# A gated block in three blocks of 1024 columns in place of four batches of 768

## The chip, the cores and the metric

One NeuronCore of a Trainium2 chip runs the whole kernel; the other cores are idle. The metric is the device time of one execution in microseconds. Engines are named as in the profile: PE (TensorE, matmuls), PEld (its weight loads), DVE (VectorE), ACT (ScalarE), POOL (GpSimd), SP (SyncE). POOL and SP only issue DMAs here, apart from some filling at the start.

## The reference

```
B, H, S, D = 4, 8, 768, 64                       # batches, heads, sequence, head size
q_bucket, k_bucket = hash bits of q @ proj, k @ proj          # 6 bits each
scores = where(q_bucket == k_bucket, q @ k^T / sqrt(D), -1e9)
attn   = softmax(scores) @ v                                  # (B, H, S, D)
x      = attn.transpose(0, 2, 1, 3).reshape(B * S, H * D)     # (3072, 512)
g      = x @ w_gate                                           # (3072, 1536)
out    = (g * sigmoid(g)) * (x @ w_val) @ w_out               # (3072, 512)
```

The inputs of attention are float32, the three weight matrices are float64 and are read as pairs of 32-bit words. Output: float32, 3072 x 512.

## The kernel before

**Attention** goes over 16 pairs of heads, numbered from 0: four pairs to a batch (`NP = 4`), since two heads of 64 rows fill the 128 partitions. For a pair n it issues the 24 score products (`score`, line 473), whose exponentials ACT writes to the ring of tiles `A` (476); DVE adds them up (`add`, 509 to 516); then come the products with v (`attend`, 487), which leave the pair's x, transposed, in a tile `xT` of 128 rows by 768 columns. The sums are taken a pair later, inverted, and spread over the partitions by two DMAs (`invert`, `r<-sums`); `norm` (551) then scales `xT`. For batches 1 to 3 the scaled x is stored to DRAM (`kept_x`, profile name `xram`, 556); for batch 0 it is split on the spot. The last pair's x is normed only in the next stage. From pair 4 on, q and k are transposed by DVE (440) and reloaded by four DMAs each (297), and the hash bits of q are copied to a second set of rows by a DMA (`qb<-qb`, 416). SP carries these DMAs in order.

In between, **pieces of the weights** are made: 36 pieces of 128 x 512, each from float64 words (`words`) by two ACT and three DVE operations (130 to 149) in a tile `stage`, then one ACT and two DVE operations (137 to 159), and stored to DRAM (`ram`, 161). 23 pieces are made during attention, the other 13 during the first batch of the next stage, by `turn`, whose steps are spread over the atoms of that stage.

**Three parts.** [...] Each operand is split into a high part h, a low part l, and a difference d. The sum of hh' and ll' goes to one PSUM tile (`a`, or the first bank of `o`), dd' to another (`n`, or the second bank), and the result is 4097 a - n. For x, `split` makes the parts: h by ACT (244), l and d by DVE (247, 251), each over 768 columns.

**The gated block** follows, with all x transposed: the token columns stream through PE and the weights are the stationary operand in the up products. For each batch b and each group f of 128 hidden columns (12 groups), `U` makes gate and value: `up` issues for both 2 x 4 x 2 matmuls into `a` and 2 x 4 into `n`, each over half a batch, 384 columns (`first`, `second`; every matmul of the stage is recorded at line 643). ACT evicts `a` (685), DVE subtracts `n` (691), ACT applies Silu (693), DVE multiplies (695), ACT rounds the product to h (696); l and d of the hidden tile `hid` follow on DVE (`tail`, 699, 701), issued after the next atom's matmuls. `D` takes three groups of `hid` at a time as stationary operands and streams three tiles of `w_out`, 512 columns wide: nine matmuls for each of six chunks of 128 tokens, into the two banks of one `o` tile. The first of the four `D` of a batch is evicted by ACT (738) and DVE (744), the others by DVE alone (740, 744); the last one's results go out by SP (746).

All PSUM is four tiles of two banks (`pp`), used in turn. Weight tiles come back from `ram` into two rings of four and three slots (`bring`, 233, POOL's queue), one load when an up product is done with its slot and three after a `D`.

The order of work is written out in the list `order`: `U` for all groups of all batches, each `D` placed after the `U` that follows the third of its groups. So the last `D` of a batch stands behind the first `U` of the next. Each `U` yields four atoms and each `D` six. The x of the next batch is loaded on SP (`load_x`, 769), two pairs before the batch's third `D` and two before its last two `U`, and split one step at a time in its last two groups. Only the very last `D` starts four of its chunks with the two older groups (`ahead`).

[...]

## Time and profile before

| | |
|---|---|
| runs | 946.80, 946.83, 948.48 us, median 946.83 |
| profiled execution | 948.66 us, span of its instructions 946.80 |
| PE, PEld, DVE, ACT, POOL busy | 927.0, 720.1, 665.1, 474.1, 112.4 us |
| first up matmul of the gated block | at 331.94 us |
| last down product | 929.35 to 941.79 us |
| mean granted clock of PE | 0.996 |
| DMA moved | 203.2 MB |

A row of operations has the line, engine and operation, output and inputs by the program's names, and sizes. A piece of the chain has its start, its length and what it was; a row of the timeline has the same and, in brackets, how long the engine had been idle and what ended that. A row by stretch has the stretch, its length, the busy time of PE, PEld, DVE, ACT and POOL with their instructions in brackets, the granted clock as a share of full speed, the mean share of the DMA engines, and GB/s.

### The profile page before, as it was taken

The numbers are of one execution on the slowest core, as the hardware profiler recorded it, in microseconds if no ns is written. First come the engines' busy times: TensorE is split into PE (matmuls) and PEld (weight loads), VectorE is DVE, ScalarE is ACT, GpSimd is POOL, SyncE is SP. The second block draws the span as 40 slices with busy tenths as digits, with TensorE's granted clock in tenths as the row PEclk, the third lists the DMA queues.
The fourth block names the chain that finished last, engine by engine and source line by source line (L and its number), as shares of the span: only waits on it lengthen the run. The fifth ranks groups of instructions, "written<-read, shape, count | busy, mean of one in ns | idle before, by whom it ended". The sixth has DMA issues, their size and how long they took to land.

```text
span 946.8 us, 14452 instructions
## 1 busy us (share of the span) xinstructions
PE 927.0 (98%) x5413; PEld 720.1 (76%) x5413; DVE 665.1 (70%) x804; ACT 474.1 (50%) x882; POOL 112.4 (12%) x223
## 2 busy tenths in 40 slices
PE   8999999999999989999999999999999999999997
PEld 4444445444444489999979999989999988999996
DVE  5566999989888738898975365676545667546466
ACT  6899878887888535535323332242331331332311
POOL 3011010001101110111011101111011011110100
PEclk9999999999999999999999999999999999999999
DMA  6466677887896598889758555467465465753741
GB/s 168 120 194 181 182 176 202 192 195 211 220 222 190 199 363 308 324 305 380 283 211 308 194 170 209 164 215 279 167 241 191 169 225 174 260 192 134 249 152 67
DMA packets 135797, 203.21 MB, mean 215 GB/s; under 512 B 92912, under 2 KB 100560, under 8 KB 135728
## 3 DMA queue, kind: packets, MB, share of 16 engines
q0 software_dynamic: 27696, 144.33, 42.8%
q1 hardware_dynamic: 107232, 57.77, 22.2%
q8 instruction: 43, 0.70, 0.3%
q10 hardware_dynamic: 800, 0.20, 0.1%
q14 instruction: 26, 0.21, 0.1%
HBM read 162.01 MB, written 39.42 MB: 213 GB/s over the span
## 4 chain that ended last, share of the span: by engine, by line
PE 84%; DVE 7%; ACT 4%; DMA 3%; issue 1%; SPq 0%; ACTq 0%; DVEq 0%; POOLq 0%
PE a L643 23%; PE o L643 19%; PE sc L473 15%; PE av L487 12%; PE n L643 12%; ACT A L476 1%; PE hps L399 1%; DVE xparts L247 1%; PE sum L527 1%; DMA r<-sums 1%; DMA xram<-xT 1%; DVE o L740 1%; DVE v L695 1%; DVE v L691 1%; ACT xparts L244 1%
## 5 line engine op out<-in xcount | busy, mean ns | idle before, releaser
L643 PE MATMUL a<-xparts,ring 128*128 128x384 f32 x1536 | 285.5, 336 | 7.9 <-ACT g L685 2.9
L643 PEld LDWEIGHTS a<-xparts,ring 128*128 128x128 f32 x1536 | 269.2, 188 | 12.0 <-ACT xparts L244 3.7
L643 PE MATMUL o<-ring,hid 128*128 128x512 f32 x864 | 199.5, 390 | 0.0
L643 PEld LDWEIGHTS o<-ring,hid 128*128 128x128 f32 x864 | 161.8, 188 | 33.6 <-DVE o L744 0.5
L476 ACT ACTIVATE A<-sc 128x384 f32<-128x384 f32 x384 | 157.4, 492 | 12.0 <-PE sc L473 12.0
L473 PE MATMUL sc<-qT,kT 64*128 64x384 f32 x768 | 158.7, 491 | 0.0
L643 PE MATMUL n<-xparts,ring 128*128 128x384 f32 x768 | 149.7, 335 | 1.1 <-DVE xparts L251 1.1
L233 POOL DMA_DIRECT2D ring<-ram x144 | 76.3, 532 | 509.8 <-PE n L643 317.9
L643 PEld LDWEIGHTS n<-xparts,ring 128*128 128x128 f32 x768 | 134.8, 188 | 2.0 <-DVE xparts L251 2.0
L487 PE MATMUL av<-A,vraw 128*64 128x386 f32 (+1 forms) x768 | 127.7, 488 | 0.0
L691 DVE TENSOR_TENSOR v<-v,n 128x768 f32<-128x768 f32 x48 | 45.7, 953 | 97.8 <-PE n L643 92.6
L685 ACT ACTIVATE g<-a 128x768 f32<-128x768 f32 x48 | 38.8, 809 | 141.3 <-PE a L643 141.3
L487 PEld LDWEIGHTS av<-A,vraw 128*64 128x64 f32 x768 | 53.7, 136 | 73.3 <-issue 64.0
L473 PEld LDWEIGHTS sc<-qT,kT 64*128 64x128 f32 x768 | 68.7, 188 | 50.2 <-issue 49.0
L696 ACT ACTIVATE hid<-v 128x768 fp32r<-128x768 f32 x48 | 40.7, 847 | 124.7 <-DVE v L695 118.9
L693 ACT ACTIVATE g<-g 128x768 f32<-128x768 f32 x48 | 40.7, 847 | 93.6 <-DVE g L691 93.6
L744 DVE TENSOR_TENSOR o<-o 128x512 f32<-128x512 f32 x90 | 61.8, 687 | 19.4 <-ACT o L738 17.1
L509 DVE SCALAR_TENSOR_TENSOR both<-A 128x1536 f32<-128x1536 f32 x32 | 56.1, 1754 | 18.3 <-ACT A L476 17.9
L473 PE MATMUL sc<-qb,kb 64*128 64x384 bf16 x384 | 64.7, 325 | 3.2 <-DMA qb<-qb 2.2
L691 DVE TENSOR_TENSOR g<-g,n 128x768 f32<-128x768 f32 x48 | 45.5, 948 | 30.2 <-PE n L643 28.7
L699 DVE SCALAR_TENSOR_TENSOR hid<-hid,v 128x768 fp32r<-128x768 f32 x48 | 45.9, 955 | 22.6 <-ACT hid L696 22.3
L740 DVE SCALAR_TENSOR_TENSOR o<-o 128x512 f32<-128x512 f32 x72 | 49.5, 688 | 13.9 <-PE o L643 13.1
(79 smaller groups left out, 727.9 us busy)
## 6 DMA issues: line engine op xcount, KB each, us to landing
ring<-ram POOLq DMA_DIRECT2D x144, 768.0 KB, 5.9
ram<-stage POOLq DMA_DIRECT2D x23, 768.0 KB, 4.9
ram<-stage SPq DMA_DIRECT2D x13, 768.0 KB
vraw<-in_v_dram SPq DMA_DIRECT2D x16, 384.0 KB
out_dram<-o SPq DMA_DIRECT2D x24, 256.0 KB
r<-sums SPq DMA_DIRECT2D x30, 192.0 KB
qraw<-in_q_dram SPq DMA_DIRECT2D x48, 96.0 KB
words<-in_moe_w_gate_dram POOLq DMA_DIRECT2D x9, 512.0 KB, 8.2
```

Source lines behind the costliest of these rows:

```text
L233: nc.gpsimd.dma_start(t.bitcast(FP32), ram[at].bitcast(FP32))
L473: nc.tensor.matmul(sc[h], x["k", n][rows, ks], x["q", n][rows, qs], start=start, stop=not start)
L476: nc.scalar.activation(weights(u)[:, h, 0:HQ], sc[h], AF.Exp, scale=SCALE * (OFF / 2 if n <= NP else 1.0))
L487: nc.tensor.matmul(ps[h * D : (h + 1) * D, 0:width], raws["v", n][:, h, c, :], a[:, h, 0:width], start=c == 0, stop=c == NCH - 1)
L509: nc.vector.scalar_tensor_tensor(out=t, in0=first, scalar=S * EPS / P / 2, in1=now, op0=ALU.add, op1=ALU.add)
L643: nc.tensor.matmul(ps, w, x, start=start, stop=stop)
L691: nc.vector.tensor_tensor(two(z), two(z), n_, op=ALU.subtract)
L693: nc.scalar.activation(z, z, AF.Silu)
L696: nc.scalar.activation(h, val, AF.Copy, scale=TOWARD / STEP)
L699: nc.vector.scalar_tensor_tensor(out=l, in0=h.bitcast(FP32), scalar=-STEP, in1=val, op0=ALU.mult, op1=ALU.add)
L740: nc.vector.scalar_tensor_tensor(out=accs[c], in0=t[:, 0], scalar=STEP + 1, in1=accs[c], op0=ALU.mult, op1=ALU.add)
L744: nc.vector.tensor_tensor(accs[c], accs[c], t[:, 1], op=ALU.subtract)
```

## The change

The columns of all batches (3072) are cut into three blocks of 1024 that run over the ends of batches; a block stands where a batch stood in the gated block. All up matmuls become 512 columns wide, and all elementwise work of an up group 1024. A `D` has eight chunks. A block's last `D` follows its last `U` directly, and every such `D` starts four chunks ahead with the two older groups; of the last block alone the other four chunks do their second product first, as before.

The parts of x now lie as two halves of 512 columns with the three parts inside. Block 0 holds batch 0 and the first 256 columns of batch 1, split during attention. For later blocks, `load_x` gathers 1024 columns from the two batches; pairs 0 and 1 are split in the last two `U` of a block, pairs 2 and 3 inside its last `D`. Their tiles take the place of block 0's parts or of the two weight stages, which now hold two pieces each.

The rings have three and three slots. The last pair's x has a tile of its own, and the spread sums for it go into an output tile. The steps of `turn` are drawn from one stream (`turns`). Pools are opened in another order, so buffers of the gated block lie elsewhere. What is scored, hashed and attended is unchanged.

```diff
+    WB = 2 * PIECE
+    NB = B * S // WB
...
-    stagep = [ctx.enter_context(tc.tile_pool(name="stagep", bufs=3))]
+    stagep = ctx.enter_context(tc.tile_pool(name="stagep", bufs=2))
...
-    even_x = ctx.enter_context(tc.tile_pool(name="even_x", bufs=1))
-    odd_x = {NP - 1: ctx.enter_context(tc.tile_pool(name="odd_x", bufs=1))}
-    RINGS = (4, 3)
+    xparts_p = ctx.enter_context(tc.tile_pool(name="xparts", bufs=1))
+    lastp = ctx.enter_context(tc.tile_pool(name="lastp", bufs=1))
+    RINGS = (3, 3)
...
+    def turns():
+        while progress["kept"] < NPIECE:
+            yield from turn()
...
-    for f in range(B * NF):
-        order.append(("U", f))
-        if f % NQ == 0 and f:
-            order.append(("D", f // NQ - 1))
-    order.append(("D", B * NF // NQ - 1))
+    for block in range(NB):
+        for f in range(NF):
+            order.append(("U", block * NF + f))
+            if f % NQ == 0 and f:
+                order.append(("D", (block * NF + f) // NQ - 1))
+        order.append(("D", (block + 1) * NF // NQ - 1))
...
+    def split(x, block, pr, first, count):
+        if (block, pr) not in xparts:
+            x_home(block, pr)
+        t = xparts[block, pr]
+        spans = []
+        at = 0
+        while at < count:
+            half, to = divmod(first + at, PIECE)
+            if to == 0 and (count - at) % PIECE == 0:
+                n = count - at
+                spans.append((x[:, at : at + n].rearrange("p (x t) -> p x t", t=PIECE),
+                              [t[:, half : half + n // PIECE, i] for i in range(3)]))
+            else:
+                n = min(PIECE - to, count - at)
+                spans.append((x[:, at : at + n], [t[:, half, i, to : to + n] for i in range(3)]))
+            at += n
...
         def low():
+            for x_, (h, l, d) in spans:
+                nc.vector.scalar_tensor_tensor(out=r32(l), in0=h, scalar=-STEP, in1=x_, op0=ALU.mult, op1=ALU.add)
...
-            else:
-                later.extend(split(x, b, pr, even_x))
+            if b * S < WB:
+                later.extend(split(x, 0, pr, b * S, min(S, WB - b * S)))
...
     def gated_block(scope):
         ringp.append(scope.enter_context(tc.tile_pool(name="late_ring", bufs=RINGS[1])))
-        rest = scope.enter_context(tc.tile_pool(name="odd_x_rest", bufs=1))
+        gatep = scope.enter_context(tc.tile_pool(name="gatep", bufs=2))
         hidp = scope.enter_context(tc.tile_pool(name="hidp", bufs=4))
-        gatep = scope.enter_context(tc.tile_pool(name="gatep", bufs=2))
         outp = scope.enter_context(tc.tile_pool(name="outp", bufs=1))
...
-                for half in halves_():
+                for half in range(WB // PIECE):
                     for j in range(NJ):
                         for v in range(2):
-                            mm(a[:, half, 0:HQ], block(v, j), xparts[b, j][:, v, halves[half]],
+                            mm(a[:, half], block(v, j), r32(xparts[b, j][:, half, v]),
...
-                    for go in (second, first) if final else (first, second):
+                    for go in (second, first) if final and c >= ahead else (first, second):
...
-                ahead = 4 if final else 0
+                ahead = 4 if part == NF // NQ - 1 else 0
...
+        def load_x(block, prs):
+            ...
+                while at < (block + 1) * WB:
+                    b, col = divmod(at, S)
+                    n = min(S - col, (block + 1) * WB - at)
+                    nc.sync.dma_start(x[:, to : to + n], kept_x[b, pr][:, col : col + n])
+        def split_x(block, pr):
+            return split(raw_x.pop((block, pr)), block, pr, 0, WB)
...
+                elif kind == "U" and f >= NF - 2:
+                    splits.extend(split_x(b + 1, f - NF + 2))
+                    if f == NF - 1:
+                        load_x(b + 1, range(NP // 2, NP))
...
+                if changing and kind == "U" and f >= NF - 2 and at:
+                    splits.pop(0)()
+                if changing and kind == "D" and f == NF // NQ - 1:
+                    if at == 0:
+                        more = [split_x(b + 1, pr) for pr in range(NP // 2, NP)]
+                        for x in more:
+                            x.pop(0)()
+                    if at in (7, 10):
+                        for x in more:
+                            x.pop(0)()
...
-                for _ in range((1, 2, 2, 2, 1, 1)[at] if kind == "U" else (1, 2, 1, 1, 1, 1, 0, 0, 0, 0)[at]):
+                for _ in range(((1, 2, 2, 2) if kind == "U" else (1, 2, 2) + (1,) * 9)[at]):
```

## The prediction

> **What bounds the kernel now.** I read the page first (busy shares, the chain that ended last), then the chain piece by piece in the gated block, then TensorE's (PE's) own instructions in order of time at each place where the chain leaves PE, and last the busy times by stretch.
>
> The page gives PE 98% of the span, and the chain lies 84% on PE. In the middle of a batch the chain is nothing else. Columns: start us, us, what.
>
> ```profile
> 518.79 2.77 PE a L643 x16
> 521.56 1.39 PE n L643 x8
> 522.95 12.28 PE o L643 x54
> ```
>
> One up product (16 matmuls into `a`, 8 into `n`, 384 columns each) takes 2.77 + 1.39 = 4.16 us, so 173.4 ns a matmul or 0.452 ns a column. A down product's 54 matmuls of 512 columns take 12.28 us: 227.4 ns, or 0.444 ns a column. These pitches, not the busy means of the groups (336 and 390 ns, which overlap), are what a matmul costs. (The granted clock of these stretches is 1.00.)
>
> The stage isn't everywhere so dense. At each change of batch PE waits for the parts of the next x, which ACT and DVE make too late (the first change; idle before the instruction in brackets):
>
> ```profile
> 474.13 1.21 PE L643 MATMUL a<-xparts,ring 128*128 128x384 f32 x6
> 476.65 0.44 PE L643 MATMUL a<-xparts,ring 128*128 128x384 f32 x1 [1.32 <-ACT xparts L244]
> 477.65 1.83 PE L643 MATMUL a<-xparts,ring 128*128 128x384 f32 x9 [0.55 <-DVE xparts L247]
> 480.37 1.15 PE L643 MATMUL n<-xparts,ring 128*128 128x384 f32 x5 [0.37 <-DVE xparts L251]
> 481.36 2.93 PE L643 MATMUL a<-xparts,ring 128*128 128x384 f32 x16
> ```
>
> The product that starts at 474.13 ends at 481.36: 7.23 us in place of 4.16, so 3.07 lost. The same reading at 626.27 to 632.90 and 777.81 to 784.43 gives 2.47 and 2.46. Sum 8.0 us.
>
> The start of the stage loses more. Chain and instructions there:
>
> ```profile
> 340.97 9.14 DMA xram<-xT
> ```
> ```profile
> 350.30 0.84 ACT L696 ACTIVATE hid<-v 128x768 fp32r<-128x768 f32 x1 [5.80 <-DMA xram<-xT]
> 351.89 4.45 PE L643 MATMUL a<-xparts,ring 128*128 128x384 f32 x16 [2.88 <-ACT g L685]
> ```
> ```profile
> 352.00:357.00 5.00, 5.00 (x20) 5.00 (x21) 4.02 (x8) 3.04 (x5) 0.00 (x0) 0.66 0.46 178
> ```
>
> The first `hid` buffer lies in memory where attention's `xT` of pair 14 lay, so ACT's write waits until that x is stored; behind it in ACT's queue stands the L685 that frees PE's PSUM tile, and PE idles 2.88 us. Then it runs 5 us at a granted clock of 0.66 (last figure but two of the stretch in the third fence; before it come the length and the busy times of PE, its weight loads, DVE, ACT and POOL): 16 matmuls take 4.45 us in place of 2.77. From 331.94, the first up matmul, to 370.24, the first down matmul, four up groups take 38.30 us in place of 8 x 4.16 = 33.3: 5.0 lost.
>
> So the gated block, 331.94 to 941.79 (last down product, 929.35 + 12.44), 609.85 us, is: 96 x 4.16 = 399.4 up, 16 x 12.28 = 196.5 down, 5.0 start, 8.0 batch changes, 0.6 in the first down product (12.85 us, DVE 12.50 of them busy), 0.4 in small edges.
>
> **The change, part by part.**
>
> *Up products 512 wide.* 2304 matmuls x 173.4 ns = 399.4 us become 3 x 12 x 2 x 24 = 1728 x 227.4 = 392.9: **6.5 us less**. The row of the down product stands for the new form, since it has the same shapes and also streams contiguous 512 columns. [...]
>
> *Evictions 1024 wide.* DVE takes 687 ns for 512 columns, 955 for 768, 1754 for 1536: about 1.04 ns a column, so an estimate of 1.22 us for 1024; ACT from 619 (512) and 847 (768), about 1.07. An up group needs 5 x 1.22 = 6.1 of DVE's time in 10.9 us of PE, against 4.8 in 8.3: no tighter. In the first block the piece work adds some 3.2 us a group (five ops of 0.42 to 0.69), 9.3 of 10.9, where before it was 7.9 of 8.3; a down product takes 16.4 us of PE in place of 12.3, so the 0.6 of the first one goes. If DVE were 5 us late, the fourth PSUM tile would stop PE.
>
> *Weights.* 108 ring loads for 144. Six slots for seven, but the shortest lead is three products, 3 x 5.46 = 16.4 us, against 5.9 us to landing. Zero on the path; only a load over 16.4 us would show.
>
> *Start.* Pools are laid out anew: `hid` now lies over attention's exponentials `A` and its sums, whose last readers are PE matmuls before 331.94. Only output tiles `o` lie over `xT`; they are first written in the first down product, 44 us on. So ACT's wait goes, and the clock's dip with it: **5.0 us less**. What takes the wait over is SP: the last pair's broadcast of 1/sum goes into an `o` tile and waits for that same store (ends 350.1), with piece stores and loads queued behind it. It is reached near 348 and lands about 10 us later (9.41 for such a transfer in the chain), before its use in the fourth group (about 370). [...] here 2.88 us of idleness was followed by 0.66. [...] I take the row, for the 16 slow matmuls are measured.
>
> *Changes of block.* Two instead of three, and the x split is moved: four x loads (eight DMAs at the first change) on SP behind nothing but piece stores, pairs 0 and 1 split during the last two up groups, pairs 2 and 3 inside the last down product, whose 16.4 us hide them. The old 8.0 goes. New is that the last down product stands directly behind its last up group and needs its `hid`. Four chunks start with the two older groups: 24 x 227.4 ns = 5.46 us of cover. The tail behind the last matmul is, by the pitches in the trace at 929.35 (0.26 to the first DVE op): v 1.22, product 1.25, ACT 1.1, low 1.25, diff 1.25, ends near 6.4 us. The first finished chunk wants diff at 5.46 + 0.45 = 5.9, so about 0.5 to 0.6 is lost, at three ends: 1.8. (The diff of x pair 1 stands on DVE ahead of low, but only while ACT works.) Then DVE does eight chunks of 1.33, two x lows and two diffs (1.22 each): about 16.7 us from the first finished chunk; the diff of pair 3 is ready about 20.8 us after the up group, PE asks at 21.2. Nothing more is lost, but here the margin is 0.4: if DVE is a microsecond late, PE is by 0.6 at two changes. **Net 8.0 - 1.8 = 6.2 less.**
>
> *End.* Before, six chunks end within 6.2 us of PE and DVE needs 1.32 each, so it ends 1.9 us after PE:
>
> ```profile
> 941.71 0.69 DVE o L740
> 942.40 0.60 DVE o L735
> 943.02 0.69 DVE o L740
> ```
>
> With eight chunks the last four come every 2.05 us, DVE catches up, and only one op of 0.69 and 0.2 of latency follow PE. **1.0 less.**
>
> *Attention.* The split of batch 0's x is now two pieces per op (512 and 256: 0.69 + 0.42 for 0.96), +0.3 us of DVE per pair; for batch 1 two ops of 0.42 on DVE and one of about 0.4 on ACT are new in four pairs. Where that hurts:
>
> ```profile
> 126.70:150.20 23.50, 21.34 (x142) 11.15 (x140) 21.38 (x22) 16.27 (x37) 1.30 (x2) 0.93 0.77 172
> 150.20:169.40 19.20, 19.20 (x138) 9.17 (x139) 17.94 (x21) 15.97 (x36) 1.30 (x2) 1.00 0.71 173
> ```
> ```profile
> 125.03 7.29 SPq L297 DMA_DIRECT2D qraw<-in_q_dram  x4
> 135.92 0.59 SPq L416 DMA_DIRECT2D qb<-qb  x1
> ```
>
> Pair 5 takes 23.5 us for 19.2: DVE, almost without a pause since 96, transposes q late, SP's reload of `qraw` waits for that, the copy of `qb` stands behind it on SP and lands at 137.8, and PE's scores wait. Two splits (at 96 and 117) are ahead of that point, so PE gets 2 x 0.3 later: **0.6 more** (bounds: 0 if the delay is absorbed, 2 if the slow clock lasts longer). In later pairs DVE has 17.9 us of 19.2, with 0.84 new it fits.
>
> Sum: -6.5 - 5.0 - 0.6 - 6.2 - 1.0 + 0.6 = **-18.7**. The profiled execution took 948.66 with a span of 946.80; the span becomes 928.1, and that execution 930.0. The median of the runs shown, 946.83, equals the span and not 948.66, so I take 946.83 - 18.7 = **928.1 us**.
>
> **Rivals.**
>
> *The start keeps its stall* (the DMA system is full there, 1.02 of its share at 340 to 352): 928.1 + 5.0 = 933.1. For it: SP now waits for the same store. Against: nothing of SP's is wanted by PE within 15 us.
>
> [...]
>
> *The block ends are not covered*: DVE is behind, and the margin of 0.4 fails: three ends at 6.4 - 0.6 more would be 17, but half of that is a DVE five microseconds late, which its load doesn't show; I put it at +6, 934.
>
> *Pair 5's stall goes* by another order on SP: -4.3, 924.
>
> *Slower:* the new DVE work pushes `qb` behind the end of `av` in every pair from 6 to 10, at pair 5's price of 4.3 us: 5 x 4.3 = 21.5, so 949.6. It decides when the transposes come 2.3 us later: the least slack is pair 7, where `qb` is issued at 173.10, lands 1.9 later, and scores start at 177.33. The new work is 0.84 a pair and DVE has over 1.2 us to spare, so it would have to pile up.
>
> That the change does nothing is excluded: the matmul count falls by 576.
>
> **How the numbers follow.** As worked out 0.70 (own range 925.5 to 931), start stall kept 0.11, width poor 0.05, ends uncovered 0.07, pair 5 cured 0.04, slower 0.03. 924.5 to 933.5 holds the first three and part of the rest, a little over 8 in 10. A difference under 0.2% (1.9 us) could not be told from none; only a mixture of rivals ends there, 0.01. Faster 0.96, slower 0.03.
>
> **What would show it.** Up products of 16 matmuls in 3.64 and 8 in 1.82 us; no wait of ACT for the x store near 350 and no clock below 0.9 there; at the ends of blocks one idle stretch of PE near 0.5 us behind DVE's diff, and none for x parts; attention ending near 332.5 in place of 331.9; DVE's last op under 1 us after PE's. Wrong would make me: a pitch over 230 ns, idle PE over 2 us at a block's end, or pairs 6 to 10 over 19.4 us.

## The result, and the profile after

| | before | after | predicted |
|---|---|---|---|
| median of the runs | 946.82 us | 932.31 us | 928.1 (924.5 to 933.5) |
| profiled execution, its span | 948.66, 946.80 | 932.62, 930.84 | span 928.1 |
| first up matmul | 331.94 | 329.66 | about 332.5 |
| gated block, first up matmul to the end of the last down product | 609.85 | 596.44 | 591.6 |
| PE's last matmul to the end of the span | 5.0 | 4.7 | 4.0 |

The changed kernel takes 0.985 of the time before (95% interval 0.982 to 0.9885); its four executions lie between 931.48 and 936.71 us. The direction and the range held; the most likely value was 4.2 us too low. The largest step, the wider up products, kept about a fifth of its size; the first down product and the end gave less than was counted; and attention differed by something that the change didn't do.

The chain that ended last, of the kernel after, in block 0 (start us, us, what):

```profile
390.31 3.63 PE a L681 x16
393.94 1.81 PE n L681 x8
...
422.95 16.32 PE o L681 x72
```

An up product takes 5.44 us here, 226.7 ns a matmul: what the row of the old down product had promised. A down product has the same pitch (16.32 us for 72).

The timeline of the kernel after (start us, us, engine, instruction, in brackets the idle time before it and what ended that):

```profile
124.86 6.07 SPq L337 DMA_DIRECT2D qraw<-in_q_dram  x4
...
135.32 0.59 SPq L456 DMA_DIRECT2D qb<-qb  x1
...
344.97 1.06 ACT L731 ACTIVATE hid<-v 128x1024 fp32r<-128x1024 f32 x1 [2.96 <-DVE v L730]
...
509.83 6.05 PE L681 MATMUL o<-ring,hid 128*128 128x512 f32 x26
516.25 10.74 PE L681 MATMUL o<-ring,hid 128*128 128x512 f32 x46 [0.36 <-DVE hid L736]
...
526.83 3.88 PE L681 MATMUL a<-xparts,ring 128*128 128x512 f32 x16
530.54 2.02 PE L681 MATMUL n<-xparts,ring 128*128 128x512 f32 x8
532.40 3.88 PE L681 MATMUL a<-xparts,ring 128*128 128x512 f32 x16
...
926.14 0.69 DVE L771 TENSOR_TENSOR o<-o 128x512 f32<-128x512 f32 x1 [0.63 <-PE o L681]
926.86 0.69 DVE L779 SCALAR_TENSOR_TENSOR o<-o 128x512 f32<-128x512 f32 x1
```

Read from the top. `qb` is issued at 135.32, 0.6 us earlier than before, not later. ACT's first `hid` waits for DVE's product and no longer for a store. At a block's end PE waits 0.36 us for DVE's `diff`, as foreseen, and for nothing of x. But the product that starts at 526.83, in block 1, ends at 532.40: 5.57 us, not 5.44. (The line of 16 is 3.88 us long and the next one starts 3.71 after it: a line's own length includes the tail of its last matmul, so products are measured from start to start.) At the end two DVE operations follow PE's last matmul, where I had counted one.

Busy times by stretch of the kernel after (length; busy PE, PEld, DVE, ACT, POOL; granted clock, DMA share, GB/s):

```profile
352.00:357.00 5.00, 5.00 (x24) 4.14 (x23) 3.81 (x5) 2.12 (x4) 0.53 (x1) 1.00 0.69 192
126.70:150.20 23.50, 22.74 (x164) 11.36 (x158) 21.73 (x24) 19.27 (x44) 1.30 (x2) 1.00 0.74 160
```

The clock is full where it was 0.66 at the start of the block, and also in attention's pair 5, where it had been 0.93.

Profiled execution against profiled execution, 948.66 to 932.62, the change is -16.0:

| term | predicted | measured |
|---|---|---|
| up products: 96 x 4.16 to 24 x 5.44 + 48 x 5.57 | -6.5 | -1.4 |
| start of the block (four groups 38.30; now 43.65 for 8 x 5.44) | -5.0 | -4.9 |
| changes of block: 8.0 to 3 x 0.7 | -6.2 | -6.0 |
| first down product: 0.4 over its matmuls (0.6 in the prediction) to 0.5 | -0.6 | +0.1 |
| down products 16 x 12.28 to 12 x 16.32, small edges | 0 | -1.2 |
| end | -1.0 | -0.3 |
| attention | +0.6 | -2.3 |

The open question is the first line: 48 of 72 up products are 0.13 us slow, although the clock is 1.00 there and DVE and ACT are less busy than in block 0 (59.18 and 26.02 of 100 us from 600 to 700, against 87.11 and 42.66 of 110 from 400 to 510). In the trace the starts of successive matmuls show a fixed pattern: in the products of block 1 the first four `n` matmuls, for x of pairs 0 to 3, take 234, 235, 231 and 227 ns, and the other four nearly the same. Pairs 0 and 1 lie in the former stage tiles there. That led to the first experiment.

### The profile page after: what moved, and what is told of

The parts are those of the page before. It is cut to its first block, busy times and chain, and to the rows that moved or that the text cites. A ratio compares the mean times of both kernels' runs of the same rounds, so it can differ in the third digit from the quotient of the medians.

```text
span 930.8 us, 13055 instructions
## 1 busy us (share of the span) xinstructions
PE 919.3 (99%) x4837; PEld 643.0 (69%) x4837; DVE 655.4 (70%) x752; ACT 467.9 (50%) x838; POOL 92.9 (10%) x187
## 4 chain that ended last, share of the span: by engine, by line
PE 86%; DVE 6%; ACT 3%; DMA 2%; issue 2%; SPq 1%; DVEq 0%; ACTq 0%; POOLq 0%
PE a L681 25%; PE o L681 18%; PE sc L512 15%; PE n L681 13%; PE av L526 12%; ACT A L515 1%; PE hps L439 1%; PE sum L565 1%; SPq L337 1%; DVE v L730 1%; DVE v L726 1%; DVE hid L734 1%; DMA r<-sums 1%; DVE hid L736 1%; PE tps L426 1%
## 5 line engine op out<-in xcount | busy, mean ns | idle before, releaser
L681 PE MATMUL a<-xparts,ring 128*128 128x512 f32 x1152 | 277.0, 392 | 0.6 <-ACT row L568 0.6
L681 PEld LDWEIGHTS a<-xparts,ring 128*128 128x128 f32 x1152 | 216.2, 188 | 50.2 <-ACT row L568 1.3
L681 PE MATMUL n<-xparts,ring 128*128 128x512 f32 x576 | 144.3, 393 | 0.0
L726 DVE TENSOR_TENSOR v<-v,n 128x1024 f32<-128x1024 f32 x36 | 43.9, 1220 | 99.7 <-PE n L681 99.7
L720 ACT ACTIVATE g<-a 128x1024 f32<-128x1024 f32 x36 | 36.9, 1025 | 127.8 <-PE a L681 121.6
L731 ACT ACTIVATE hid<-v 128x1024 fp32r<-128x1024 f32 x36 | 38.2, 1061 | 115.1 <-DVE v L730 115.1
L728 ACT ACTIVATE g<-g 128x1024 f32<-128x1024 f32 x36 | 38.2, 1062 | 81.8 <-DVE g L726 81.8
L726 DVE TENSOR_TENSOR g<-g,n 128x1024 f32<-128x1024 f32 x36 | 43.7, 1215 | 34.6 <-PE n L681 34.6
L734 DVE SCALAR_TENSOR_TENSOR hid<-hid,v 128x1024 fp32r<-128x1024 f32 x36 | 44.0, 1223 | 22.8 <-ACT hid L731 22.8
L551 DVE TENSOR_TENSOR both<-both,A 128x1536 f32<-128x1536 f32 x32 | 56.3, 1758 | 3.3
```

What stands on the lines that cost most here:

```text
L551: nc.vector.tensor_tensor(t, t, now, op=ALU.add)
L681: nc.tensor.matmul(ps, w, x, start=start, stop=stop)
L726: nc.vector.tensor_tensor(two(z), two(z), n_, op=ALU.subtract)
L728: nc.scalar.activation(z, z, AF.Silu)
L731: nc.scalar.activation(h, val, AF.Copy, scale=TOWARD / STEP)
L734: nc.vector.scalar_tensor_tensor(out=l, in0=h.bitcast(FP32), scalar=-STEP, in1=val, op0=ALU.mult, op1=ALU.add)
```

## The experiments

"Place" below is a tile's address within a partition, modulo the number given. In both kernels all of `xparts`, `ring` and `hid` lie at 416 modulo 512 bytes, except the two stage tiles of the changed kernel, which lie at 128. The expectations speak of this as 32 and 0 modulo 128; a later run showed that 128 is not the period. Where no ratio stands behind a time below, the kernel ran once; there the argument rests on the products in its trace, and the whole time can be off by the 3 us that attention varies.

**Stage tiles moved by 288 bytes.**

```diff
-    stagep = ctx.enter_context(tc.tile_pool(name="stagep", bufs=2))
     small = ctx.enter_context(tc.tile_pool(name="small", bufs=3))
+    stagep = ctx.enter_context(tc.tile_pool(name="stagep", bufs=2))
```

> The changed kernel with the pool of small tiles laid ahead of the stage pool: the two stage tiles, which hold x parts of pairs 0 and 1 in the second block and of pairs 2 and 3 in the third, move by 288 bytes (from 28800 and 41088 to 29088 and 41376 in each partition, so from 0 to 32 in units modulo 128 bytes, where all other tiles that TensorE reads lie); nothing else moves and no instruction changes. Theory 'placement' (matmuls that stream from a tile at 0 modulo 128 are slower, and the delay spills into the next ones): the products of the second and third block go from 5.57 to 5.44 us, 48 x 0.13 = 6.2 us, so 926.1. Rival 'region, data or neighbours' (low addresses, the values of later x, or what other engines do then): still 5.57 us, 932.3.

Measured: 926.59 us, 0.9782 of the kernel before (0.9764 to 0.98). Its timeline at the same place as above:

```profile
527.23 3.79 PE L681 MATMUL a<-xparts,ring 128*128 128x512 f32 x16
530.86 1.98 PE L681 MATMUL n<-xparts,ring 128*128 128x512 f32 x8
532.67 3.79 PE L681 MATMUL a<-xparts,ring 128*128 128x512 f32 x16
```

5.44 us in all three blocks, and the gated block takes 591.45 us, against 591.6 by the prediction's steps. That this agrees so well is in part luck: the first down product lost 1.65 us in this execution, and down products and small edges took 1.2 less than was assumed. No instruction differs. The slow pitch is one of place.

**x tiles moved to where the stage tiles were.**

```diff
-    small = ctx.enter_context(tc.tile_pool(name="small", bufs=3))
     xparts_p = ctx.enter_context(tc.tile_pool(name="xparts", bufs=1))
+    small = ctx.enter_context(tc.tile_pool(name="small", bufs=3))
```

> The changed kernel with the pool of small tiles laid behind the x tiles: all x tiles of the first block move from 32 to 0 modulo 128 bytes (by 288 bytes), where the stage tiles already are; weights (ring) and hid stay at 32. Theory 'placement': all up products of all blocks are slow now, each of 24 matmuls at 234 or 235 ns and more, 5.6 us or more a product, the first block too; 24 products of the first block lose 0.2 us or more each and the 48 others 0.05 or more: 936 to 942 us. Rival 'region, data or neighbours': first block stays at 5.44, others at 5.57, 932.3.

Measured: 940.39 us. Its timeline in block 0:

```profile
393.52 3.90 PE L681 MATMUL a<-xparts,ring 128*128 128x512 f32 x16
397.25 2.03 PE L681 MATMUL n<-xparts,ring 128*128 128x512 f32 x8
399.12 3.89 PE L681 MATMUL a<-xparts,ring 128*128 128x512 f32 x16
```

5.60 us a product in every block, the starts 232 and 235 ns apart in turn. Not the low addresses and not the data, then. The down products, whose operands didn't move, stay at 16.3.

**x tiles at three places.** Tiles 0 and 1 get 32 bytes more, so that what follows shifts: the x tiles lie 64, 32, 0 and 0 bytes short of the weights' place.

```diff
+    def x_tile(i):
+        size = WB // PIECE * 3 * PIECE
+        t = xparts_p.tile([P, size + (8 if i < NP // 2 else 0)], FP32, tag=f"x{i}", name="xparts")
...
-            t = xparts_p.tile([P, WB // PIECE, 3, PIECE], FP32, tag=f"x{pr}", name="xparts")
+            t = x_tile(pr)
```

> The changed kernel with x tiles 0 and 1 longer by 32 bytes, so the x tiles lie at 32, 64, 96 and 96 modulo 128 bytes, weights (ring) and hid at 96, stage tiles at 0 as in the changed kernel. Theory 'only 0 modulo 128 is slow': the first block stays at 226.7 ns for every matmul, second and third as in the changed kernel (234 or 235 ns on stage tiles), 932. Rival 'every multiple of 64': matmuls that read x tile 1 (at 64) take 234 or so in the first block. Rival 'the distance between moving tile and weights': reads of tiles 2 and 3 (same offset as the weights) take 226.7, others differ, and the down products, both operands at 96 modulo 128, stay at 226.7.

Measured: 939.61 us; six products of block 0 take 33.48 us, 5.58 each, while the down products stay at 16.3. "Only 0 is slow" fell: nothing of block 0 lies there. "Every multiple of 64" is not needed and wasn't excluded by this run. The rival "distance" did not fit matmul by matmul either: those of tiles 2 and 3, at the weights' own place, took 227 to 236 ns. In the changed kernel, too, matmuls from a good tile that follow bad ones take up to 236 ns before they come back to 227. A delay is carried on, so a mixed product can't be read one matmul at a time, and the next runs keep a product pure.

**Weights at two places.** The pool of small tiles goes behind the first three ring slots; x, stage tiles and slots 1 to 3 share one place, slots 4 to 6 and `hid` another.

```diff
-    small = ctx.enter_context(tc.tile_pool(name="small", bufs=3))
...
     ringp = [ctx.enter_context(tc.tile_pool(name="ringp", bufs=RINGS[0]))]
+    small = ctx.enter_context(tc.tile_pool(name="small", bufs=3))
```

> The changed kernel with the pool of small tiles laid behind the first three ring slots: x and stage tiles and ring slots 1 to 3 lie at 0 modulo 128 bytes, ring slots 4 to 6 and hid at 32. Theory 'distance' (a matmul is slow when the tile that streams and the tile its weights come from lie at different places modulo 128 bytes): up products with weights from slots 1 to 3 take 5.44 us, those from slots 4 to 6 about 5.60, three by three; in the down products matmuls that stream from slots 1 to 3 (hid is the weights there) are slow and those from 4 to 6 at 226.7 ns. Rival 'the streamed tile at 0 is slow, wherever the weights lie': all up products 5.60.

Measured: 934.27 us. Its timeline in block 0, where the second product of the five lines takes its weights from slot 4:

```profile
340.41 3.79 PE L681 MATMUL a<-xparts,ring 128*128 128x512 f32 x16
344.04 1.98 PE L681 MATMUL n<-xparts,ring 128*128 128x512 f32 x8
345.86 3.89 PE L681 MATMUL a<-xparts,ring 128*128 128x512 f32 x16
349.58 2.03 PE L681 MATMUL n<-xparts,ring 128*128 128x512 f32 x8
351.45 3.90 PE L681 MATMUL a<-xparts,ring 128*128 128x512 f32 x16
```

345.86 - 340.41 is 5.45 us, 351.45 - 345.86 is 5.59; over the kernel products change between 5.44 and 5.60 with the ring slot, three by three. The down products, which stream from these slots, take 16.67 to 16.72. x lies at the same address in fast and slow products: it is the distance between the streamed tile and the weights that counts.

**How far, and modulo what.** x and stage tiles all at one place, ring and `hid` 64 bytes further, and in another kernel 128 bytes further (a gap of 32 words in place of 16, and two buffers of small tiles in place of three).

```diff
     small = ctx.enter_context(tc.tile_pool(name="small", bufs=3))
     stagep = ctx.enter_context(tc.tile_pool(name="stagep", bufs=2))
...
+    gap = ctx.enter_context(tc.tile_pool(name="gap", bufs=1))
+    gap.tile([P, 16], FP32, tag="gap", name="gap")
     ringp = [ctx.enter_context(tc.tile_pool(name="ringp", bufs=RINGS[0]))]
```

> The changed kernel with all x and stage tiles at 32 modulo 128 bytes and ring and hid at 96, so 64 apart in every up product and 0 apart in every down product. If the distance counts modulo 64: all products 5.44, down 16.32, 926. If it counts modulo 128: all 72 up products about 5.58 to 5.60, 10 to 11 us more, 937. Rival 'the weights' own place' (at 96 in the run with stepped x tiles, where the first block was slow): up slow too, but then the down products, whose weights lie at 96 as well, would be slow, which they were not in that run.

> As in the run with the weights 64 bytes off, but with 128: all x and stage tiles at 320 modulo 512 bytes, ring and hid at 448 (the pool of small tiles has two buffers in place of three, to make room). In all runs so far the fast products had streamed tile and weights at the same place even modulo 512 bytes, and the slow ones were 32 or 64 bytes off, so the period isn't known yet. If it is 128: all up products 5.44 us, 926. If it is 256 or 512: all 5.60, 937. Down products 16.32 in both.

Measured: 939.31 and 937.89 us. The timeline of the second:

```profile
346.77 3.88 PE L683 MATMUL a<-xparts,ring 128*128 128x512 f32 x16
350.48 2.02 PE L683 MATMUL n<-xparts,ring 128*128 128x512 f32 x8
352.33 3.89 PE L683 MATMUL a<-xparts,ring 128*128 128x512 f32 x16
```

5.60 us in nearly every product of both (a few of the second take 5.56 to 5.59), and 16.34 in the down products, whose operands moved together. So 64 and even 128 bytes are not a period. In all fast products of all runs the distance is a whole multiple of 512 bytes; 256 was not tried. Why a distance costs 6.7 ns a matmul is not shown by any of this.

**The width.** On the kernel with the stage tiles moved, block 1 is cut to 256 columns and block 2 to 384 and 128.

```diff
+            cuts = ((0, 512), (0, 256, 512), (0, 384, 512))[b]
...
-                            mm(a[:, half], block(v, j), r32(xparts[b, j][:, half, v]),
+                            mm(a[:, half, to], block(v, j), r32(xparts[b, j][:, half, v, to]),
```

> The changed kernel with stage tiles at 32 modulo 128 bytes; the up matmuls stay 512 wide in the first block, are cut to 256 columns in the second, and to 384 and 128 in the third. Theory 'a fixed cost of 13.3 ns beside the columns': 227 ns at 512, 173 at 384, 120 at 256, 67 at 128, so a product of the second block takes 48 x 120 = 5.76 us and of the third 24 x (173 + 67) = 5.76, and the whole 24 products x 2 x 0.32 = 15 us more (942). Rival 'the load of the next weights sets the pitch where the columns are few' (a load takes about 187 ns by the records, or less where they overlap)[...]; with 187 a product of the second block takes 9.0 us, 1011 us. [...]

Measured: 970.93 us. Its timeline in block 1:

```profile
539.96 4.00 PE L681 MATMUL a<-xparts,ring 128*128 128x256 f32 x32
543.80 2.08 PE L681 MATMUL n<-xparts,ring 128*128 128x256 f32 x16
545.72 4.00 PE L681 MATMUL a<-xparts,ring 128*128 128x256 f32 x32
```

48 matmuls in 5.76 us, 120.0 ns each. So 120.0, 173.4 and 226.7 ns at 256, 384 and 512 columns: 0.417 ns a column and 13.3 ns beside them in all three. At 128 columns the theory failed. In block 2:

```profile
746.43 4.75 PE L681 MATMUL a<-xparts,ring 128*128 128x384 f32 x32
751.01 2.25 PE L681 MATMUL n<-xparts,ring 128*128 128x384 f32 x14
```

A line of the view has one form for both widths: its 32 matmuls are 16 pairs of 384 and 128. From start to start they take 4.58 us, 286 ns a pair, so about 113 for the narrow one, where 67 was expected. Whether the weight load sets that is not shown.

**The start of the block, alone.** The kernel before, with its pools in the order of the changed kernel, so that `hid` lies over no `xT`.

```diff
+        fixed = scope.enter_context(tc.tile_pool(name="fixed", bufs=1))
         att = scope.enter_context(tc.tile_pool(name="att", bufs=2))
         xp = scope.enter_context(tc.tile_pool(name="xp", bufs=4))
-        fixed = scope.enter_context(tc.tile_pool(name="fixed", bufs=1))
...
+        gatep = scope.enter_context(tc.tile_pool(name="gatep", bufs=2))
         rest = scope.enter_context(tc.tile_pool(name="odd_x_rest", bufs=1))
...
         hidp = scope.enter_context(tc.tile_pool(name="hidp", bufs=4))
-        gatep = scope.enter_context(tc.tile_pool(name="gatep", bufs=2))
```

> The kernel before, with only its pools in another order, so that the first hid buffer no longer lies over the xT whose store ends near 350 (attention's constants and exponentials lie below its sums and xT, gate tiles ahead of the x parts and of hid). Theory of the prediction: ACT's wait near 350 and the 0.66 clock go, four up groups take 33.3 us in place of 38.3; 5.0 us less, 941.8. Rival 'the stall moves' (to the o tiles of the first down product, or into the first down product, where DVE is short): 944 to 946.8. Its attention is that of the kernel before, so its profile also shows how pair 5's stall (23.5 us for 19.2, slow clock after it) repeats: theory 'the changed kernel's attention gained 2.3 us by the change': first up matmul at 331.9 again; rival 'the profiled execution of before had a longer stall than most': at about 330.

Measured: 944.06 us, 0.997 of the kernel before (0.9957 to 0.9983). The four up groups take 35.29 us: 3.0 of the 5.0 are gone and 2.0 stay. Its timeline:

```profile
338.37 1.02 DVE L551 SCALAR_TENSOR_TENSOR xT<-xT,e,r 128x768 f32<-128x768 f32 x1 [12.28 <-DMA r<-sums]
...
342.99 3.07 PE L643 MATMUL a<-xparts,ring 128*128 128x384 f32 x16 [0.42 <-ACT v L685]
...
345.58 0.85 ACT L696 ACTIVATE hid<-v 128x768 fp32r<-128x768 f32 x1 [2.65 <-DVE v L695]
...
352.09 3.05 PE L643 MATMUL a<-xparts,ring 128*128 128x384 f32 x16 [0.46 <-ACT v L685]
```

ACT's first `hid` waits for DVE and no longer for the store. But DVE stands idle for 12.28 us ahead of the norm of the last pair but one, whose spread sums arrive late, and everything DVE and ACT owe the first groups is late by that. With 4.16 us a product PE catches up with them three times, and such a wait costs more than its idle time, by what is called a restart here: with 0.42 idle ahead of 342.99, the product from 338.24 takes 4.75 us in place of 4.16. In the changed kernel DVE stands there nearly as long (10.79 us, until 336.73), and PE, with 5.44 us a product, doesn't wait. So of the 5.0 the place of `hid` earned 3.0; the other 2.0 went only in the whole change. That the wider products did it is argued from these lengths; no run has them alone.

Its attention has the same instructions as before's, and here the first up matmul comes at 329.81, not 331.94.

**Pair 5's stall.** The copy of `qb` issued from ACT's queue.

```diff
-                nc.sync.dma_start(bits["q", n][high], bits["q", n][low])
+                nc.scalar.dma_start(bits["q", n][high], bits["q", n][low])
```

> The changed kernel with the copy of the qb sign bits issued from ACT's queue, right behind the ACT instruction that writes them, in place of SP's, where it stands behind the reload of qraw. Theory 'pair 5's stall is SP's queue': TensorE's two waits for qb of 0.8 us and the lengthened pair 5 go, pair 6's av starts near 145.2 in place of 147.9, first up matmul near 327 in place of 329.7; 2 to 3 us less, 929.5. Rival 'ACT pays': the issue holds ACT about 0.6 us a pair ahead of the exponentials' turn, TensorE waits for sc's eviction in each pair, and the gain is lost or turned: 932 to 938.

Measured: 932.06 us, 0.9837 (0.9822 to 0.9852): nothing gained that can be told from the changed kernel's 932.31. The wait for `qb` is gone, but the chain shows what stood just behind it:

```profile
134.06 0.96 DVE acc L554
...
135.05 0.42 DVE kb L453
135.50 0.42 DVE kb L453
...
136.05 9.22 PE sc L512 x68
```

`kb` comes from DVE, which adds the exponentials' sums without a pause until 135.0; that is about when SP issued `qb` in the changed kernel (135.32). Neither theory held whole: the queue was one of two late things. (ACT did not pay in every pair: pairs from 6 on take 19.23 as before.) The two intervals discussed below take 39.8 us here.

With all runs at hand, the two intervals that hold the stall (from 106.8 to about 148) take 43.4 and 41.2 us with the attention of before, and 40.3, 40.4, 40.5, 40.7, 41.0, 41.1, 42.0, 42.5, 43.3 and 43.5 with that of the changed kernel. The same instructions differ by 3 us. SP's four reloads of `qraw` take 6.07 us of issue in one execution and 7.42 in another, and `qb` follows. Where PE then waited 1.1 us or less at a time, the clock stayed full. After waits of 1.55 to 2.16 us it was 0.50 for 3.41 us in four runs (in before from 138.16 to 141.57), but not in the run with 64 bytes, after 2.00; the last section has the stretches.

**Half the cover at a block's end.**

```diff
-                ahead = 4 if part == NF // NQ - 1 else 0
+                ahead = (4 if final else 2) if part == NF // NQ - 1 else 0
...
-                    if at in (7, 10):
+                    if at in (5, 8):
```

> The changed kernel with two chunks in place of four begun with the two older groups in a block's last down product, at the first and second end (the last end keeps four). The cover for the last hid falls from 24 to 12 matmuls, 5.46 to 2.73 us. Theory of the prediction (the first chunk is held by diff, 6.4 us behind the last up matmul): TensorE waits 0.36 + 2.73 = 3.1 us at these two ends in place of 0.36, the down product with its gap takes 19.7 in place of 17.0, and the run 5.5 us more, 937.8. Rival 'l and h hold it as well': the wait splits in two, same sum. Rival 'the wait is not diff's alone' (DVE's other work): the wait grows by less than 2.5 or by more than 3.5.

Measured: 942.78 us, 10.5 more. Timeline, and then the busy times by stretch behind it (columns as above, granted clock last but two):

```profile
513.25 0.50 PE L681 MATMUL o<-ring,hid 128*128 128x512 f32 x1 [1.01 <-ACT hid L731]
514.51 0.73 PE L681 MATMUL o<-ring,hid 128*128 128x512 f32 x1 [0.76 <-DVE hid L734]
515.76 16.10 PE L681 MATMUL o<-ring,hid 128*128 128x512 f32 x58 [0.53 <-DVE hid L736]
```
```profile
512.20:515.70 3.50, 1.27 (x3) 0.41 (x2) 3.47 (x3) 2.90 (x3) 0.00 (x0) 0.84 0.40 169
515.70:519.00 3.30, 3.23 (x8) 2.59 (x9) 2.34 (x5) 0.00 (x0) 0.00 (x0) 0.50 0.04 14
519.00:521.00 2.00, 2.00 (x6) 1.59 (x5) 0.34 (x1) 0.00 (x0) 0.00 (x0) 0.50 0.64 240
521.00:523.00 2.00, 2.00 (x9) 1.60 (x8) 1.30 (x2) 0.00 (x0) 0.00 (x0) 0.89 0.00 0
```

The first `d` matmul comes 515.76 - 509.35 = 6.41 us behind the last up matmul, against 6.42 in the changed kernel: the model of the tail (ends near 6.4) holds to the hundredth, and the wait is divided over h, l and d as the first rival said. The price was wrong. The gap (2.3 us idle, in three parts, and restarts) brings the clock down to 0.50 for about 6.8 us, by the means of these stretches from about 514.6, in the middle of the gap, to 521.4; the 58 matmuls from 515.76 take 15.9 us in place of 13.1. A down product with its gap takes 22.35 us, 5.35 more, twice what the idle time says.

**The old order of the last down product.**

```diff
-            if f % NQ == 0 and f:
+            if f % NQ == 0 and block + f:
                 order.append(("D", (block * NF + f) // NQ - 1))
-        order.append(("D", (block + 1) * NF // NQ - 1))
+    order.append(("D", NB * NF // NQ - 1))
...
-                ahead = 4 if part == NF // NQ - 1 else 0
+                ahead = 4 if final else 0
...
-                if changing and kind == "D" and f == NF // NQ - 1:
...
+                if changing and (kind, f) == ("U", NF - 1) and at == 3:
+                    finish(splits)
+                    more = [split_x(b + 1, pr) for pr in range(NP // 2, NP)]
+                    for x in zip(*more):
+                        finish(list(x))
```

> The changed kernel with the last down product of the first and second block put back behind the next block's first up group, as in the kernel before; the x parts of pairs 2 and 3 are then split right behind the last up group, ahead of the next one. Theory of the prediction (the direct order hides the split): the 0.5 to 0.7 of TensorE's wait behind hid's diff goes at two ends, and the first up product of the next block waits for ACT's and DVE's parts of pairs 2 and 3, four DVE operations of 1.22 and hid's product ahead of them, 3 to 6 us at each of two changes; 6 to 10 us more in sum, 938 to 942. Rival 'the order is worth little' (ACT and DVE are idle enough to have them in time): under 2 us in sum.

Measured: 946.24 us, its span 13.6 longer than that of the changed kernel. Its timeline at the first change:

```profile
514.51 0.50 PE L681 MATMUL a<-xparts,ring 128*128 128x512 f32 x1 [3.74 <-ACT xparts L283]
515.77 5.34 PE L681 MATMUL a<-xparts,ring 128*128 128x512 f32 x11 [0.76 <-DVE xparts L287]
```

At the two changes one up product takes 13.60 and 12.63 us in place of 5.57, 8.0 and 7.1 more; the two ends give 0.7 each back. The 4.5 us of idle time shown are what the theory had; most of the rest is again the clock: 0.76 in the mean of 512 to 518, 0.50 from 518 to 522 and 1.00 behind that, so 0.50 for about 6.9 us from about 515.1. This is not the split of before, which began two groups earlier and lost 2.5 to 3.1 a change; it is what the split costs in this place without its cover.

**All that the runs suggested.** Stage tiles moved; in a block's last down product `d` is asked for later; the very last chunk's subtrahend in a PSUM tile of its own; no weight piece begun in pair 4.

```diff
...
+                            for x in range(c + 1 if c else 0, min(c + 2, ahead)):
+                                go, late[x] = start(x, [NQ - 1])
+                                go()
+                            late.pop(c)()
+                            end(c)
...
+                        if final and c == NCB - 1:
+                            other = two_banks("o")
+                            start(c, range(NQ), other)[1]()
+                            nc.vector.tensor_tensor(accs[c], accs[c], other[:, 1], op=ALU.subtract)
+                            start(c, range(NQ))[0]()
+                            end(c, True)
...
-        PACE = [2] * 4 + [1] * 3 + [2, 1] * 4 + [0]
+        PACE = [2] * 4 + [0] + [1] * 2 + [2, 1] * 4 + [0]
```

> The changed kernel with the stage tiles at 32 modulo 128 bytes (926.6 measured), and three edits, each read at its own place of the trace. (a) In a block's last down product the last hid of the first four chunks comes as: h and l matmuls of chunks 0 and 1, d of 0, h and l of 2, d of 1, and so on, so d is asked for 0.9 us after the two older groups' 5.46 us, and not 0.45. Theory (diff is late by 0.36 us plus 0.11 of restart): TensorE's wait behind diff goes at the three ends, 0.5 to 0.6 each, 1.6 in sum; rival: the fifth chunk then waits for the first one's PSUM tile, 0.2 or more, and half or all of it is lost. (b) The very last chunk's subtrahend has a PSUM tile of its own and comes first, so one DVE op of 0.69 in place of two (1.41) follows the last matmul: 0.7 less from the last matmul to the end (4.7 to 4.0); rival: the end is the output transfer's, no gain. (c) Pair 4 begins no weight piece (five DVE ops less there, one piece more in the first block). Theory 'DVE is late at pairs 4 and 5': pairs 5 and 6, 41.1 us together in the changed kernel and 38.5 at the pace of later pairs, come to under 39; rival 'SP's queue': 40 or more. All three: 922.5 to 923.5; rivals only: 926.

Measured: 924.18 us, 0.976 of the kernel before (0.9744 to 0.9776), the fastest version. Timeline:

```profile
508.73 16.89 PE L681 MATMUL o<-ring,hid 128*128 128x512 f32 x72
...
918.29 0.69 DVE L775 SCALAR_TENSOR_TENSOR o<-o 128x512 f32<-128x512 f32 x1
```

(a) A block's last down product takes 16.73, from 16.99: 0.25 gained at each of three ends, not 0.5. The line has no idle time long enough to be marked, but the starts of the matmuls show two hitches of 0.19 and 0.16, at the first `d` and at the fifth chunk, which waits for the first one's tile: the rival took half. (b) DVE ends 0.80 us after PE in place of 1.45, yet the span ends 4.42 after it in place of 4.75: half was given back by the output transfer (3.62 from DVE's last operation to the end of the span, 3.29 in the changed kernel). (c) The two intervals take 39.3 us, the least seen, with no wait for `qb`; this lies between the two theories' numbers, and next to executions that spread by 3 us one profile doesn't settle it.

## Why the prediction was right or wrong

- **Up products 512 wide (-6.5): mechanism right, size wrong by 5.1.** The pitch is 226.7 ns as taken from the row of the down product, and the 13.3 ns beside the columns are the same at 256, 384 and 512. ("Width poor" among the chances was my estimate, with no row behind it.) What failed is that the row stood for *all* new products: its operands lie 512-byte-even to each other, those of blocks 1 and 2 don't. The change moves two x tiles to the stage tiles' addresses, and I looked at which buffers they share, not at where these lie. With those two tiles moved by 288 bytes, all products take 5.44 us and give the predicted gain.
- **Start (-5.0): right, -4.9; its reason was half the story.** Where the wait for the store was said to be all of it, it is 3.0. The other 2.0 came from DVE's lateness, which PE meets with narrow products and not in the changed kernel. The rival that the stall stays is refuted.
- **Changes of block (-6.2): right, -6.0.** Three waits of 0.36 behind DVE's `diff` with a restart, 0.7 in all where I had 0.6. The tail's 6.4 us held. What a thinner cover costs was priced too low: 2.3 us of idle time brought 2.8 more at a clock of 0.50. (One sum is off without effect: eight chunks of 1.33 and four splits of 1.22 are 15.5 us of DVE, not 16.7. The diff of pair 3 was done at 530.66 and asked for near 531.2, so the thin margin held.)
- **First down product (-0.6): failed.** In the kernel before there was only 0.4 to lose, for the 12.85 is the length of a row, with the tail of its last matmul; from start to start it is 12.69:

```profile
370.24 12.85 PE L643 MATMUL o<-ring,hid 128*128 128x512 f32 x54
382.93 2.96 PE L643 MATMUL a<-xparts,ring 128*128 128x384 f32 x16
```

  In the changed kernel it still loses 0.5 in this execution (0.20 of it a wait behind DVE's `o`), and 0.2 to 1.7 in the others with the same work there. That 16.4 us of PE would hide DVE's 12.5 was not enough of an argument; I did not look at what DVE still owed when the product began.
- **End (-1.0): failed by 0.7.** "One op of 0.69 and 0.2 of latency": both of the last chunk's DVE operations come behind the chunk's last matmul, though the subtrahend is computed first. In the trace the subtrahend's last matmul ends at 924.75 and DVE is free from 925.52, but its first operation starts at 926.14, 0.04 behind the end of PE's last matmul. 1.45 follow, not 0.9. In the last run, where the subtrahend has a tile of its own, its operation starts at 917.50, 0.68 ahead of that end. And the output transfer took 3.29 where it took 3.04.
- **Attention (+0.6): wrong in sign, but not by the change.** The same program differs by 3 us from one execution to the next there, and the profiled execution of before was one of the long ones. The term should have been "0, and 1.5 either way".
- **The sum against which time.** I took -18.7 from the median because it happened to equal the span. The executions are 1.8 us longer than their spans in both kernels, and before's profiled one was 1.8 above its median. This base error of +1.8 offsets most of attention's -2.9, so the total looks better than its terms: in part the range held by luck.
- **What would make me wrong** included "a pitch over 230 ns". That is what happened, in two blocks of three; it was listed, with no mechanism and no chance of its own. The slower rival (`qb` late in pairs 6 to 10) didn't occur: 19.23 us each.

## What to carry to other kernels

A duration taken from a row holds for the same operands at the same relative place: when a change moves a matmul's streamed tile or its weights, write both addresses down and compare them modulo 512 bytes before you reuse a pitch (here 226.7 ns and 233.3). Before you cost a stall, compare several executions of the same program at that point, if there are any, and put a stall that comes and goes into the range and not into the sum. Add the slow clock to the cost of TensorE's waits: here it stood at 0.50 for 3.41 us or about 6.8 behind waits of 1.55 to 4.5 us in all, though not behind each, which is up to 1.7 or 3.4 us beside the idle time (an estimate: half of these lengths). And look for what stands second in line before you remove what stands first.

## What the runs showed of the hardware that was not expected

- **The distance between a matmul's two SBUF tiles.** With streamed tile and weights a multiple of 512 bytes apart in the partition, a 512-wide matmul with its weight load took 226.7 ns (5.44 us for 24); 64, 128 or 288 bytes off it took 233.3 on average (5.60), 3% more. Where half of a product's matmuls were 288 bytes off, it took 5.57: nearly all was lost. With x at 128 modulo 512 a product took 5.45 us with weights at 128 and 5.59 with weights at 416; with both at 416 it took 5.44, so the place itself made no difference. On 1728 matmuls the two pitches come to some 11 us, an estimate.
- **The slow clock.** In the traces of before and after the granted clock is 1.00 or 0.50. In before it fell to 0.50 twice while PE had work, at 138.16 and 353.20, each time for 3.41 us, and a third time at 947.12, behind the last instruction. The falls are 215.04 and 593.92 us apart, 63 and 174 times 3.413. The stretches of that length around the first two, and one that holds PE's last matmul and ends 173 times 3.413 behind the second fall:

```profile
134.75:138.16 3.41, 1.25 (x8) 0.54 (x10) 2.24 (x5) 0.94 (x2) 0.00 (x0) 1.00 0.59 96
138.16:141.57 3.41, 3.41 (x15) 2.08 (x14) 3.31 (x6) 1.66 (x4) 0.37 (x1) 0.50 0.33 106
```
```profile
349.79:353.20 3.41, 1.31 (x7) 1.31 (x8) 1.99 (x3) 2.06 (x3) 0.05 (x1) 1.00 1.03 420
353.20:356.61 3.41, 3.41 (x13) 3.41 (x12) 2.59 (x5) 2.59 (x4) 0.00 (x0) 0.50 0.31 113
```
```profile
940.29:943.71 3.42, 1.50 (x7) 0.92 (x5) 3.32 (x6) 0.00 (x0) 0.00 (x0) 1.00 0.54 204
943.71:946.70 2.99, 0.00 (x0) 0.00 (x0) 0.01 (x1) 0.00 (x0) 0.00 (x0) 1.00 0.31 117
```

  PE was busy for 1.25 and 1.31 us of 3.41 ahead of the two falls. With 1.50 of 3.42 the clock stayed full, and so it did at the first change of batch, where PE idles 1.32, 0.55 and 0.37 us between 475 and 481. In the run with 64 bytes PE waited 2.00 us for `qb`, nearly the 2.16 of before, and the clock stayed full too:

```profile
127.00:137.00 10.00, 9.63 (x65) 3.77 (x57) 8.94 (x8) 6.86 (x15) 0.00 (x0) 1.00 0.73 124
137.00:143.00 6.00, 4.38 (x33) 3.07 (x34) 4.76 (x10) 3.85 (x10) 0.53 (x1) 1.00 0.39 93
```

  So waits of about 2 us were followed by either. Which idle time brings the fall, and what sets the distances, is not shown by these runs.
- **128 columns.** Matmuls 128 wide, each with its own weight load, took about 113 ns (run with cut widths), where 0.417 ns a column and 13.3 give 67.
